# Statistics, row scales and branches rearranged between an attention stage and a gated feed-forward stage

## The chip, the cores and the metric

One core of one Trainium2 chip. The metric is the device time of one execution in microseconds (us); lower is better. The kernel before has a median of 538.29 us over 3 runs (535.64 to 538.82).

## The reference, cut to what matters

```python
def reference(**kw):
    attn_out = _attn_ref(q, k, v, n_global, n_local)   # B 2, H 8, S 768, D 64: local window and global keys
    x = attn_out.transpose(0, 2, 1, 3).reshape(B * S, H * D)       # 1536 x 512
    x = _moe_ref(x, w_gate, w_val, w_out, rms_g)
    return _moe2_ref(x, w_skip, w_gate, w1, w2)        # 8 experts, one for each token

def _moe_ref(x, w_gate, w_val, w_out, rms_g):
    rms = np.sqrt(np.mean(x * x, axis=-1, keepdims=True) + 1e-06)
    xn = x / rms * rms_g
    g = xn @ w_gate                                    # 512 x 1536
    silu = g * (1.0 / (1.0 + np.exp(-g)))
    return silu * (xn @ w_val) @ w_out
```

The change lies where the attention ends and `_moe_ref` begins: the root mean square over each row of x, and the first columns of the two products with `w_gate` and `w_val`.

## The kernel before, in words

Four stages follow each other: the attention (to about 85 us), the gated products with `w_gate` and `w_val` (to about 290 us), the product with `w_out` together with the routing (to about 408 us), and the experts. The program's order is written out by hand: each engine runs its instructions in the order in which the code issues them.

**Attention.** `attention` is a generator that goes over 24 items (head pair, group of 256 rows) in a software pipeline: in turn t it issues the scores of item t, the transposes (`trans`) of item t-2, the products with v (`pv`) of item t-3 and the output (`out`) of item t-4. Turns 24 to 27 drain the pipeline. `out` calls `Rms.take`: the item's output, which lies transposed (features on partitions, tokens on columns), is scaled by `rms_g`, split into a high part `xh` and a low part `xl`, and squared (`sq`); GpSimd adds the squares up (L398).

**Sum and root.** `Rms.stats` sums the squares over the features with TensorE: the 128x128 block of squares is the weight and one column of ones is the moving operand, so each call gives one column of `ss`. The 14 such matmuls appear in the trace as 28 instructions (two passes of 32-bit data). `root` computes 1/sqrt on a 128x12 tile in 12 small VectorE instructions. The scale is needed along the columns, as 1536 columns on all partitions (`rs`, three tiles of 512). `spread` makes them: a column of r, broadcast as weight, times the identity, 12 matmuls (24 passes), six copies to `rs` by ScalarE (L463).

**Gated products.** x has three tiles of 512 columns (index c); the 1536 gate columns are 12 pieces of 128 (index i), each with a gate and a value half (z = 0, 1). `products(i, c, a, b)` issues 24 matmuls, 12 for each z, each into its own PSUM tile (tags `ps0` and `ps1`, two buffers each). `gate1` evacuates them: VectorE multiplies the gate half by `rs` (L538), ScalarE takes the SiLU (L540), VectorE multiplies by the value half (L542). A PSUM buffer comes free with that, so products two pieces later wait for a gate. From piece (1, 0) on, a loop over `order` runs products, the splitting of a next weight unit, and the gate of the piece before.

**Weights.** Weights come as 64-bit floats. `load_unit` issues a 512 KB DMA from SP's queue into one of two buffers `wraw`; `split_unit` turns it into a high and a low 32-bit half in seven steps (ScalarE L471, VectorE L473, L478, L480, L483, ScalarE L485, GpSimd L486). The second buffer is free again behind L483.

**Filling.** In the drain, 12 of the 24 matmuls of piece (0, 0) (`s.first`) are issued as filling, six in turn 24 and six in turn 26 (`FILL`). The stats follow in turns 26 and 27. Behind the attention come the other 12 matmuls of (0, 0), `root`, then half pieces of c = 1 and the six `spread` calls in turns.

**Branches.** `flag` chooses a general attention where the mask is wide. It isn't taken with these inputs. It is read three times: before the attention, at turn 16 (L1029), and behind the attention (L1040).

Of the kernel before, what the change touches and what calls it, by code (L numbers as in the profile page):

```python
# [8 lines left out]
F32 = mybir.dt.float32  # L9
# [7 lines left out]
AX = mybir.AxisListType  # L17
PSUM = bass.MemoryType.PSUM
NEG = -1.0e9
FILL = {0: 6, 2: 6}  # L20
FAST_LOCAL = 97
FAST_GLOBAL = 32
FAR = 1 << 20
# [166 lines left out]
def attention(s, rms):  # L190
# [6 lines left out]
    nc, ap = s.nc, s.apool  # L197
# [79 lines left out]
    def trans(it, r):  # L277
        pr, g = it
        e = st[it][1]
        pt = s.ps_n.tile([128, 3, 128], F32, name="pt", tag="rb", bufs=2)  # L280
        for k in range(1 if g == r == 0 else 0, 3):
            nc.tensor.transpose(pt[:, k, :], e[:, r, 128 * k:128 * k + 128], s.ident)
        pts = ap.tile([128, 3, 128], F32, name="pts", bufs=4)
        outs[it, r] = (pt, pts)
# [40 lines left out]
    n = len(items)  # L325
# [12 lines left out]
    for t in range(n + 4):  # L338
        a, b, c, d, e = (items[t - z] if 0 <= t - z < n else None for z in range(5))
        if a:  # L340
            qk(a, t)
        if c:
            trans(c, 0)
            trans(c, 1)
        if d:
            pv(d, 0)
            pv(d, 1)
        some(s.first, FILL.get(t - n, 0))
        if b:
            zadd(b)  # L350
            zrec(b)
            for r in range(2):
                for x in range(2):
                    if t < n or r == 0:
                        norm(b, r, x, nc.gpsimd)
        if a:
            ttr(a, 0, 0)
        if a:
            ttr(a, 0, 1)
            ttr(a, 1, 0)  # L360
        if b and t >= n:
            norm(b, 1, 0, nc.vector)
            norm(b, 1, 1, nc.vector)
        if a:
            ttr(a, 1, 1)
        if c:
            evac(c, 0, nc.vector)
        if e:
            out(e)
        for half in range(2):  # L370
            if a:
                exp(a, half)
        if c:
            evac(c, 1, nc.scalar)
        if a:
            pr, g = a
            if g == 1 and pr + 2 < 8:
                load(pr + 2)
            if g == 2 and pr + 2 < 8:
                loadv(pr + 2)  # L380
        yield t


class Rms:
# [16 lines left out]

    def parts(self, hp, g, x, sq):
        s, nc = self.s, self.s.nc
        k, c = place(3 * self.b + g)
        nc.scalar.activation(s.xh[k][:, hp, c], x, AF.Copy, scale=s.rg[:, hp:hp + 1])
        nc.scalar.activation(sq, x, AF.Square)
        nc.vector.scalar_tensor_tensor(out=s.xl[k][:, hp, c], in0=x, scalar=s.rg[:, hp:hp + 1],
                                       in1=f(s.xh[k][:, hp, c]), op0=ALU.mult, op1=ALU.subtract)
# [17 lines left out]
    def stats(self, g, ss):  # L426
        s, nc = self.s, self.s.nc
        sqs = self.sq if g == 2 else self.sq[:1]
        for j in range(2 * g, 2 * g + 2):
            for z, sq in enumerate(sqs):  # L430
                nc.tensor.matmul(ss[:, 6 * self.b + j:6 * self.b + j + 1], lhsT=sq[:, 128 * j:128 * j + 128],
                                 rhs=s.ones[:, 0:1], start=z == 0, stop=z == len(sqs) - 1)


def place(z):

    return z // 2, slice(256 * (z % 2), 256 * (z % 2) + 256)


def root(s, ss):  # L440
# [11 lines left out]
        nc.vector.scalar_tensor_tensor(out=r, in0=t, scalar=1.5, in1=r, op0=ALU.add, op1=ALU.mult)  # L452


def spread(s, z):

    nc = s.nc
    rb = s.bank([128, 256], "rb")
    for j in range(2):
        nc.tensor.matmul(rb[:, 128 * j:128 * j + 128], lhsT=s.r[:, 2 * z + j:2 * z + j + 1].to_broadcast([128, 128]),  # L460
                         rhs=s.ident, start=True, stop=True)
    k, c = place(z)
    nc.scalar.copy(s.rs[k][:, c], rb)  # L463


def unpack(s, raw, pool, hi, lo, eng):
# [22 lines left out]
def load_unit(s, unit):  # L489

    raw = s.wpool.tile([128, 512, 2], I32, name="wraw", bufs=2)
    src = s.w_out[128 * unit[1]:128 * unit[1] + 128, :] if unit[0] == "o" else \
        s.wgv[unit[1], :, 512 * unit[2]:512 * unit[2] + 512]
    s.nc.sync.dma_start(raw.rearrange("p n t -> p (n t)"), src.bitcast(I32))
    s.wraw[unit] = raw
# [14 lines left out]
def products(s, i, c, a, b):  # L510

    nc = s.nc
    ps = []
    for z in range(2):
        p = s.ps_g.tile([128, b - a], F32, name=f"ps{z}", bufs=2)
        wh, wl = s.w[i, z]
        n = 0
        for k in range(4):
            for w, x in ((wh, s.xh), (wh, s.xl), (wl, s.xh)):
                nc.tensor.matmul(p, lhsT=w[:, k, :], rhs=x[c][:, k, a:b], start=n == 0, stop=n == 11)  # L520
                n += 1
                yield
        ps.append(p)
    s.gp[i, c, a, b] = ps


def some(parts, n):

    for _ in range(n):
        next(parts, None)  # L530


def gate1(s, i, c, a, b):

    nc = s.nc
    ps = s.gp.pop((i, c, a, b))
    u = s.h[c, i // 2][:, i % 2, a:b]
    nc.vector.tensor_tensor(u, ps[0], s.rs[c][:, a:b], ALU.mult)  # L538
    sg = s.gpool.tile([128, b - a], F32, name="sg", bufs=2)
    nc.scalar.activation(sg, u, AF.Silu)  # L540
    yield
    nc.vector.tensor_tensor(u, sg, ps[1], ALU.mult)  # L542
# [177 lines left out]
def run(*parts):  # L720

    parts = list(parts)
    while parts:
        parts = [p for p in parts if next(p, FAR) is None]
# [213 lines left out]
def attn_moe_kernel(ctx, tc, qx, kx, vx, rel, ints, wgv, w_out, rms_g, w9, w9t, w1, w2, out):  # L938
    s = K()
    nc = s.nc = tc.nc  # L940
# [4 lines left out]
    def pool(stack, name, side=None, space=None):  # L945
        kw = {} if space is None else {"space": space}
        return stack.enter_context(
            tc.tile_pool(name=name, bufs=1, side=side, reuse_waits="tile", **kw))

    s.cpool = pool(ctx, "const")  # L950
    dram = pool(ctx, "dram", space=bass.MemoryType.DRAM)
    s.xg = dram.tile([1024, 768], F32, name="xg")
    s.xm = dram.tile([1536, 512], F32, name="xm")
    ctx.enter_context(tc.manual_schedule())

    phase1, phase2 = ExitStack(), ExitStack()
    rctx, actx, gctx = ExitStack(), ExitStack(), ExitStack()
    s.gpool = pool(phase2, "g")
    early = pool(phase2, "early")
    s.apool = pool(actx, "attn")  # L960
# [2 lines left out]
    def htiles(pool, c, qs):  # L963
        for q in qs:
# [3 lines left out]
    rms = [Rms(s, 0), Rms(s, 1)]  # L968
# [15 lines left out]
    flag = nc.values_load(s.fasti[0:1, 0:1], min_val=0, max_val=1,  # L984
                          skip_runtime_bounds_check_because="a comparison's result")
# [9 lines left out]
        s.rs[c] = xpool.tile([128, 512], F32, name=f"rs{c}")  # L995
    s.rpool = pool(rctx, "rms", side="right")
    ps_n = s.ps_n = pool(gctx, "ps_n", space=PSUM)
    ps_o = pool(actx, "ps_o", space=PSUM)
    s.banks = 0

    def bank(shape, name):
# [17 lines left out]
    unit = unpacked()  # L1019
    s.first = products(s, 0, 0, 0, 512)  # L1020
    for t in att:
        if t < 3:
            next(bias)
        if t == 4:
            load_unit(s, units[0])
            load_unit(s, units[1])
        if 9 <= t < 19 or t > 23:
            next(unit, None)
        if t == 16:  # L1029
            with tc.If(flag == 0):  # L1030
                rms[0].general(s.xg)
        if t == 26:
            ss = s.ps_n.tile([128, 12], F32, name="ss", tag="rb", bufs=2)
            for g in range(3):
                rms[0].stats(g, ss)
            rms[1].stats(0, ss)
            rms[1].stats(1, ss)
        if t == 27:
            rms[1].stats(2, ss)
    with tc.If(flag == 0):  # L1040
        rms[1].general(s.xg)
        for g in range(3):
            rms[1].stats(g, ss)


    some(unit, 2)
    some(s.first, 24)
    root(s, ss)
    second = products(s, 0, 1, 0, 256)
    some(second, 12)  # L1050
    spread(s, 0)
    spread(s, 1)
    gate = gate1(s, 0, 0, 0, 512)
    next(gate)
    spread(s, 2)
    some(second, 24)
    run(gate)
    for z in range(3, 6):
        spread(s, z)
    run(gate1(s, 0, 1, 0, 256))  # L1060
    run(products(s, 0, 1, 256, 512))
    run(unit)
    run(products(s, 0, 2, 0, 512))
    run(gate1(s, 0, 1, 256, 512))
    behind = [(0, 2, 0, 512)]
    rctx.close()
    actx.close()
# [6 lines left out]
    htiles(big, 0, range(1, 6))  # L1074
    htiles(big, 1, range(1, 6))
    htiles(big, 2, range(6))
    order = [(i, c, 0, 512) for i in range(1, 12) for c in range(3)]
    todo = {(i, c, 0, 512): [("w", i + 1, c)] for i in range(1, 11) for c in range(2)}
    places = [(i, 2, 0, 512) for i in (1, 2, 3, 4, 4, 5, 6, 7, 7, 8, 9, 10)]
    for n, x in enumerate(places):  # L1080
        todo.setdefault(x, []).append(("o", n))
    ahead = iter([unit for x in order for unit in todo.get(x, ())])
    for _ in range(2):
        load_unit(s, next(ahead))

    def step1(x, *parts):

        run(products(s, *x))
# [1 line left out]
        behind.append(x)  # L1090

    for x in order:
        if x == order[-1]:
            run(gate1(s, *behind.pop()))
            xctx.close()
            hctx = ExitStack()
            s.hspool = pool(hctx, "hs")
            s.hs = {}
            split_h(s, 0)
        step1(x, *[split_unit(s, unit, nc.gpsimd) for unit in todo.get(x, ())])  # L1100
        for unit in todo.get(x, ()):
            unit = next(ahead, None)
            if unit:
                load_unit(s, unit)
# [57 lines left out]
    rows = (1, 5)  # L1162
# [293 lines left out]
```

## Time and profile before

| | us |
|---|---|
| median of 3 runs | 538.29 |
| lowest, highest | 535.64, 538.82 |
| the profiled execution, its own time | 538.66 |
| its span, first to last instruction | 536.8 |

The page gives the busy time of each engine over the span, and the span in 40 slices; other views give windows of time, the waits of an engine with what ended them, single instructions in order of time, and the DMA issues with their time to landing. A line as "79.45 0.52 PE L282 ... x3 [0.68 <-ACT pts L293]" says: at 79.45 us TensorE began three instructions of line 282 that together took 0.52 us, and before them it was idle 0.68 us until ScalarE's L293 ended. Matmuls are pipelined, so their durations overlap; a pace is read from the starts. TensorE is shown busy at either clock, so the granted clock has to be read beside it.

### The profile page before, as it was taken

The page shows a single profiled execution, that of the slowest core. Times are in us where ns is not written, and L with a number is a line of the kernel's source. Part 1 is how long each engine was busy: PE and PEld are TensorE (multiplying, and loading weights), DVE is VectorE, ACT ScalarE, POOL GpSimd, SP SyncE. Part 2 cuts the span into 40 slices and gives each one's busy share as a digit, 9 for nine tenths or more (in the row PEclk, how much of TensorE's full clock was granted, in tenths as well). Part 3 has the DMA queues.
Part 4 walks back from the last instruction along what each step waited for, and adds up shares of the span by engine and source line. Part 5 has one row for each costly group of instructions (what it writes and reads, how often), then busy time and mean ns, then how long its engine had stood idle before and what let it go on. Part 6 is the DMA issues. An engine that isn't in the chain of part 4 may idle for free. (4 is left out here: it accounts for less than half of the span.)

```text
span 536.8 us, 9708 instructions
## 1 busy us (share of the span) xinstructions
PE 514.3 (96%) x3376; PEld 417.8 (78%) x3376; DVE 396.4 (74%) x991; ACT 269.0 (50%) x621; POOL 150.6 (28%) x202
## 2 busy tenths in 40 slices
PE   3998989999999999999999999999999999999994
PEld 2676768888888888888888887887898778888873
DVE  6889985378887688768855367767743699999961
ACT  3899993432323333233323434424521778988750
POOL 5477782021221222222212000000000613666001
PEclk9999998999999999999999999999999999999998
DMA  8798701022222332232306123223681899999200
GB/s 263 251 333 260 238 16 40 12 96 92 100 97 78 117 119 87 92 129 87 117 29 233 74 78 119 82 75 118 211 307 39 293 398 397 397 402 395 100 14 17
DMA packets 30999, 85.91 MB, mean 160 GB/s; under 512 B 3847, under 2 KB 4103, under 8 KB 30944
## 3 DMA queue, kind: packets, MB, share of 16 engines
q1 hardware_dynamic: 26400, 73.86, 39.9%
q0 software_dynamic: 2672, 8.22, 4.1%
q10 hardware_dynamic: 1872, 3.15, 1.7%
q8 instruction: 28, 0.46, 0.4%
q14 instruction: 27, 0.22, 0.1%
HBM read 77.52 MB, written 8.65 MB: 161 GB/s over the span
## 5 line engine op out<-in xcount | busy, mean ns | idle before, releaser
L520 PE MATMUL ps<-xh,wh 128*128 128x512 f32 (+1 forms) x296 | 114.9, 388 | 0.1
L520 PE MATMUL ps<-xl,wh 128*128 128x512 f32 (+1 forms) x296 | 114.4, 387 | 0.0
L520 PE MATMUL ps<-xh,wl 128*128 128x512 f32 (+1 forms) x296 | 114.3, 386 | 0.0
L850 DVE TENSOR_TENSOR ewl<-eraw,ewh 128x1024 fp32r<-128x1024 f32 x72 | 83.4, 1216 | 7.6 <-ACT ewh L841 7.4
L841 ACT CAST ewh<-eraw 128x1024 fp32r<-128x1024 f32 x72 | 71.4, 1055 | 6.5 <-DVE ewl L850 4.6
L520 PEld LDWEIGHTS ps<-xh,wh 128*128 128x128 f32 x296 | 56.3, 190 | 11.5 <-issue 0.2
L520 PEld LDWEIGHTS ps<-xl,wh 128*128 128x128 f32 x296 | 56.2, 190 | 11.1
L520 PEld LDWEIGHTS ps<-xh,wl 128*128 128x128 f32 x296 | 56.2, 190 | 11.0
L473 DVE SCALAR_TENSOR_TENSOR wraw<-f64t,wraw 128x512 f32<-128x512 f32 x36 | 43.7, 1214 | 25.4 <-ACT f64t L471 25.4
L600 PE MATMUL px<-woh,hh 128*128 128x512 f32 (+1 forms) x156 | 61.2, 392 | 0.0
L486 POOL TENSOR_TENSOR wl<-f64t,wh 128x512 fp32r<-128x512 f32 x24 | 31.0, 1294 | 105.8 <-ACT wh L485 67.2
L600 PE MATMUL px<-woh,hl 128*128 128x512 f32 (+1 forms) x156 | 58.4, 374 | 0.0
L600 PE MATMUL px<-wol,hh 128*128 128x512 f32 (+1 forms) x156 | 58.2, 373 | 0.0
L485 ACT CAST wh<-f64t 128x512 fp32r<-128x512 f32 x24 | 14.9, 622 | 74.9 <-DVE f64t L483 74.9
L258 ACT ACTIVATE es<-es,m 128x192 f32<-128x192 f32 (+1 forms) x96 | 41.4, 445 | 5.6 <-DVE m L247 5.5
L275 POOL TENSOR_SCALAR es<-es,z 128x192 f32<-128x192 f32 (+1 forms) x94 | 37.8, 420 | 16.6 <-DVE z L267 6.3
L554 DVE TENSOR_TENSOR hl<-h,hh 128x256 fp32r<-128x256 f32 x72 | 25.4, 421 | 17.8 <-ACT hh L553 17.8
L542 DVE TENSOR_TENSOR h<-sg,ps 128x512 f32<-128x512 f32 (+1 forms) x37 | 24.7, 667 | 14.6 <-PE ps L520 10.7
L600 PEld LDWEIGHTS px<-woh,hh 128*128 128x128 f32 x156 | 29.4, 188 | 5.5 <-issue 0.9
L600 PEld LDWEIGHTS px<-woh,hl 128*128 128x128 f32 x156 | 29.3, 188 | 5.5
L600 PEld LDWEIGHTS px<-wol,hh 128*128 128x128 f32 x156 | 29.4, 189 | 4.1
L538 DVE TENSOR_TENSOR h<-ps,rs 128x512 f32<-128x512 f32 (+1 forms) x37 | 24.9, 672 | 10.3 <-ACT rs L463 5.7
(199 smaller groups left out, 986.5 us busy)
## 6 DMA issues: line engine op xcount, KB each, us to landing
eraw<-in_w_dram SPq DMA_DIRECT2D x64, 512.0 KB, 11.0
wraw<-in_wgv_dram SPq DMA_DIRECT2D x24, 512.0 KB, 3.8
wraw<-in_w_out_dram SPq DMA_DIRECT2D x12, 512.0 KB, 3.2
vp<-in_vx_dram SPq DMA_DIRECT2D x8, 704.0 KB, 6.0
eraw<-in_w_dram POOLq DMA_DIRECT2D x8, 512.0 KB, 13.5
kd<-in_kx_dram SPq DMA_DIRECT2D x7, 464.0 KB, 9.0
xm<-x SPq DMA_DIRECT2D x12, 256.0 KB, 2.8
out_dram<-x ACTq DMA_DIRECT2D x12, 256.0 KB
```

What stands on the lines that cost most here:

```text
L258: nc.scalar.activation(e[:, r, e0:e0 + n], e[:, r, e0:e0 + n], AF.Exp, bias=m[:, j:j + 1], scale=-1.0, accum_out=z[:, j:j + 1])
L275: eng.tensor_scalar(e[:, r, e0:e0 + n], e[:, r, e0:e0 + n], z[:, j:j + 1], one[0], ALU.mult, *one[1:])
L473: nc.vector.scalar_tensor_tensor(out=a.bitcast(F32), in0=t, scalar=F64_LEAST, in1=a.bitcast(F32), op0=ALU.is_ge, op1=ALU.mult)
L485: nc.scalar.copy(hi, t)
L486: eng.tensor_tensor(lo, t, f(hi), ALU.subtract)
L520: nc.tensor.matmul(p, lhsT=w[:, k, :], rhs=x[c][:, k, a:b], start=n == 0, stop=n == 11)
L538: nc.vector.tensor_tensor(u, ps[0], s.rs[c][:, a:b], ALU.mult)
L542: nc.vector.tensor_tensor(u, sg, ps[1], ALU.mult)
L554: nc.vector.tensor_tensor(hl[:, i, :], src, f(hh[:, i, :]), ALU.subtract)
L600: nc.tensor.matmul(p, lhsT=h[:, k, :], rhs=w[k][:, c:c + N], start=n == 0, stop=n == 35)
L841: eng.copy(wh, raw)
L850: eng.tensor_tensor(wl, raw, f(wh), ALU.subtract)
```

## The change

- The filling moves: three matmuls of `s.first` between the two transposes of turn 24, seven behind the products with v of turn 24, none in turn 26 as a block. Instead, one matmul of `s.first` stands behind each of the 14 stats matmuls. With 3 + 7 + 10 + 4 = 24 all of piece (0, 0) is issued inside the attention.
- `spread` changes from 12 matmuls and six copies to one transpose of r (128x12), one copy to SBUF by VectorE, one DMA of 6 KB to DRAM and three DMAs of 256 KB that read it back to all partitions, all on SP's queue.
- The rest of the splitting (`run(unit)`) and the next two weight loads stand ahead of `root`; before, most of this stood between and behind the gates.
- The two halves of piece (0, 1) get one PSUM bank each (`half0`, `half1`), piece (0, 2) takes the two banks of the attention's output, so four pieces stand in PSUM before the first gate. All gates follow behind the products of (0, 2).
- The branch of turn 16 joins the one behind the attention.

The text of the change also names 384-column exponentials; the diff has no line on the exponentials.

```diff
-FILL = {0: 6, 2: 6}
@@ attention, turn t
         if c:
             trans(c, 0)
+            if t == n:
+                some(s.first, 3)
             trans(c, 1)
         if d:
             pv(d, 0)
             pv(d, 1)
-        some(s.first, FILL.get(t - n, 0))
+        if t == n:
+            some(s.first, 7)
@@ Rms.stats, behind each matmul
+                yield
@@
-def spread(s, z):
+def spread(s):
     nc = s.nc
-    rb = s.bank([128, 256], "rb")
-    for j in range(2):
-        nc.tensor.matmul(rb[:, 128 * j:128 * j + 128], lhsT=s.r[:, 2 * z + j:2 * z + j + 1].to_broadcast([128, 128]),
-                         rhs=s.ident, start=True, stop=True)
-    k, c = place(z)
-    nc.scalar.copy(s.rs[k][:, c], rb)
+    p = s.ps_n.tile([12, 128], F32, name="rp", tag="rb", bufs=2)
+    nc.tensor.transpose(p, s.r, s.ident)
+    rows = s.rpool.tile([12, 128], F32, name="rows", bufs=1)
+    nc.vector.tensor_copy(rows, p)
+    nc.sync.dma_start(s.rd, rows)
+    for k in range(3):
+        nc.sync.dma_start(s.rs[k].rearrange("p (a b) -> p a b", a=4),
+                          s.rd[4 * k:4 * k + 4, :].rearrange("(o a) b -> o a b", o=1).to_broadcast([128, 4, 128]))
@@ attn_moe_kernel
-        if t == 16:
-            with tc.If(flag == 0):
-                rms[0].general(s.xg)
         if t == 26:
             ss = s.ps_n.tile([128, 12], F32, name="ss", tag="rb", bufs=2)
+            for x, g in ((0, 0), (0, 1), (0, 2), (1, 0), (1, 1)):
+                for _ in rms[x].stats(g, ss):
+                    some(s.first, 1)
+        if t == 27:
+            for _ in rms[1].stats(2, ss):
+                some(s.first, 1)
+    with tc.If(flag == 0):
+        for x in rms:
+            x.general(s.xg)
             for g in range(3):
-                rms[0].stats(g, ss)
-            rms[1].stats(0, ss)
-            rms[1].stats(1, ss)
-        if t == 27:
-            rms[1].stats(2, ss)
...
-    some(unit, 2)
-    some(s.first, 24)
+                run(x.stats(g, ss))
+        run(products(s, 0, 0, 0, 512))
+    run(unit)
...
+    for _ in range(2):
+        load_unit(s, next(ahead))
     root(s, ss)
-    second = products(s, 0, 1, 0, 256)
-    some(second, 12)
-    spread(s, 0)
-    spread(s, 1)
-    gate = gate1(s, 0, 0, 0, 512)
-    next(gate)
-    spread(s, 2)
-    some(second, 24)
-    run(gate)
-    for z in range(3, 6):
-        spread(s, z)
-    run(gate1(s, 0, 1, 0, 256))
-    run(products(s, 0, 1, 256, 512))
-    run(unit)
+    for z in range(2):
+        pair = s.ps_g.tile([128, 2, 256], F32, name=f"half{z}", tag=f"ps{z}", bufs=2)
+        s.gp[0, 1, 256 * z, 256 * z + 256] = [pair[:, x, :] for x in range(2)]
+    s.gp[0, 2, 0, 512] = [s.bank([128, 512], "po") for _ in range(2)]
+    run(products(s, 0, 1, 0, 256))
+    second = products(s, 0, 1, 256, 512)
+    some(second, 6)
+    spread(s)
+    some(second, 18)
     run(products(s, 0, 2, 0, 512))
-    run(gate1(s, 0, 1, 256, 512))
+    for x in ((0, 0, 512), (1, 0, 256), (1, 256, 512)):
+        run(gate1(s, 0, *x))
     behind = [(0, 2, 0, 512)]
```

## Rows read from the trace of the kernel before

**Rows 1.** The page's first part: busy time, share of the span, instructions.

```profile
PE 514.3 (96%) x3376; PEld 417.8 (78%) x3376; DVE 396.4 (74%) x991; ACT 269.0 (50%) x621; POOL 150.6 (28%) x202
```

**Rows 2.** Windows: length, busy us (instructions) by engine, clock, DMA share, GB/s.

```profile
110.00:180.00 70.00, 70.00 (x310) 57.97 (x309) 54.57 (x76) 21.70 (x38) 16.79 (x13) 1.00 0.30 98
430.00:500.00 70.00, 69.68 (x336) 56.81 (x335) 69.52 (x91) 58.16 (x75) 32.52 (x12) 1.00 1.03 394
```

**Rows 3.** TensorE's longest wait from 110 us to the end: us, times, longest.

```profile
PE rk L696 <- DVE oh L659: 0.7, 2, 0.4
```

**Rows 4.** TensorE's matmuls in order of time: start, us, instructions, idle before them.

```profile
79.45 0.52 PE L282 MATMUL pt<-ident,es 128*128 128x128 f32 x3 [0.68 <-ACT pts L293]
...
86.50 0.28 PE L431 MATMUL ss<-ones,sq 128*128 128x1 f32 x2
...
90.49 0.77 PE L520 MATMUL ps<-xh,wh 128*128 128x512 f32 x1
...
95.72 0.28 PE L520 MATMUL ps<-xh,wh 128*128 128x256 f32 x1
...
97.15 0.38 PE L460 MATMUL rb<-ident,r 128*128 128x128 f32 x2
...
98.69 0.36 PE L520 MATMUL ps<-xh,wh 128*128 128x256 f32 x1
...
100.19 1.83 PE L460 MATMUL rb<-ident,r 128*128 128x128 f32 x12
101.78 0.36 PE L520 MATMUL ps<-xh,wh 128*128 128x256 f32 x1
...
104.73 0.40 PE L520 MATMUL ps<-xh,wh 128*128 128x512 f32 x1
...
110.20 0.39 PE L520 MATMUL ps<-xh,wh 128*128 128x512 f32 x1
```

**Rows 5.** Windows for `ss` (PE, PEld, DVE) and all tiles (also ACT, POOL); clock, DMA.

```profile
88.00:88.50 0.50, 0.50 (x7) 0.50 (x6) 0.00 (x0) 1.00 0.00 0
89.00:89.50 0.50, 0.50 (x4) 0.50 (x4) 0.00 (x0) 0.50 0.34 115
96.00:97.00 1.00, 1.00 (x11) 1.00 (x10) 0.00 (x0) 0.00 (x0) 0.00 (x0) 1.00 0.00 0
```

**Rows 6.** ScalarE and VectorE in order of time, behind the attention.

```profile
88.49 0.66 ACT L471 ACTIVATE f64t<-wraw 128x512 f32<-128x512 f32 x1
...
90.47 0.17 DVE L444 TENSOR_SCALAR rv<-ss 128x12 f32<-128x12 f32 x1 [2.54 <-PEq L1040]
...
92.73 0.17 DVE L452 SCALAR_TENSOR_TENSOR r<-rt,r 128x12 f32<-128x12 f32 x1
...
98.63 1.28 ACT L540 ACT_TABLE_LOAD   x1
98.64 0.69 DVE L538 TENSOR_TENSOR h<-ps,rs 128x512 f32<-128x512 f32 x1 [5.74 <-ACT rs L463]
```

**Rows 7.** Two steps of the splitting: duration in ns, least, median, greatest.

```profile
L473 DVE SCALAR_TENSOR_TENSOR wraw<-f64t,wraw x36: 682/1352/1677, 39.4 to 270.4; 128x512 f32<-128x512 f32 x36
...
L480 DVE SCALAR_TENSOR_TENSOR f64t<-wraw,f64t x36: 674/693/695, 45.5 to 272.7; 128x512 uint32<-128x512 uint32 x36
```

**Rows 8.** The first DMA of 2 KB: issue, and the instruction that waited for it.

```profile
0.79 0.41 SPq L40 DMA_DIRECT2D ints<-in_ints_dram  x1
...
4.10 0.17 DVE L60 CAST intw<-ints 128x4 f32<-128x4 int32 x1 [4.10 <-DMA ints<-in_ints_dram]
```

**Rows 9.** Line 605, 256 KB to DRAM, 12 times: issue to landing, us.

```profile
DMA to landing us min/median/max: 2.4/2.8/5.1
```

**Rows 10.** DMA issues: count, KB each, median us from issue to landing.

```profile
vlo<-in_vx_dram SPq DMA_DIRECT2D x8, 192.0 KB, 9.4
```

**Rows 11.** ScalarE in turn 16, either side of its branch.

```profile
58.65 0.48 ACT L293 COPY pts<-pt 128x384 f32<-128x384 f32 x1
59.25 0.47 ACT L405 ACTIVATE xh<-po,rg 128x256 fp32r<-128x256 f32 x1
```

More of the change, by code (lines that the diff above doesn't have):

```diff
@@ L403, in parts @@
         s, nc = self.s, self.s.nc
-        k, c = place(3 * self.b + g)
+        n = 3 * self.b + g
+        k, c = n // 2, slice(256 * (n % 2), 256 * (n % 2) + 256)
         nc.scalar.activation(s.xh[k][:, hp, c], x, AF.Copy, scale=s.rg[:, hp:hp + 1])
@@ L432, in stats @@
                                  rhs=s.ones[:, 0:1], start=z == 0, stop=z == len(sqs) - 1)
-def place(z):
-    return z // 2, slice(256 * (z % 2), 256 * (z % 2) + 256)
+                yield
 def root(s, ss):
@@ L512, in products @@
     nc = s.nc
-    ps = []
+    ps = s.gp.setdefault((i, c, a, b), [])
     for z in range(2):
-        p = s.ps_g.tile([128, b - a], F32, name=f"ps{z}", bufs=2)
+        if z == len(ps):
+            ps.append(s.ps_g.tile([128, b - a], F32, name=f"ps{z}", bufs=2))
+        p = ps[z]
         wh, wl = s.w[i, z]
@@ L522, in products @@
                 yield
-        ps.append(p)
-    s.gp[i, c, a, b] = ps
 def some(parts, n):
@@ L953, in attn_moe_kernel @@
     s.xm = dram.tile([1536, 512], F32, name="xm")
+    s.rd = dram.tile([12, 128], F32, name="rd")
     ctx.enter_context(tc.manual_schedule())
     phase1, phase2 = ExitStack(), ExitStack()
-    rctx, actx, gctx = ExitStack(), ExitStack(), ExitStack()
+    rctx, actx, octx, gctx = ExitStack(), ExitStack(), ExitStack(), ExitStack()
     s.gpool = pool(phase2, "g")
@@ L997, in attn_moe_kernel @@
     ps_n = s.ps_n = pool(gctx, "ps_n", space=PSUM)
-    ps_o = pool(actx, "ps_o", space=PSUM)
+    ps_o = pool(octx, "ps_o", space=PSUM)
     s.banks = 0
@@ L1028, in attn_moe_kernel @@
             next(unit, None)
-        if t == 16:
-            with tc.If(flag == 0):
-                rms[0].general(s.xg)
         if t == 26:
             ss = s.ps_n.tile([128, 12], F32, name="ss", tag="rb", bufs=2)
-            for g in range(3):
-                rms[0].stats(g, ss)
-            rms[1].stats(0, ss)
-            rms[1].stats(1, ss)
-        if t == 27:
-            rms[1].stats(2, ss)
[L1040 to L1043, printed above, removed]
@@ new lines, in attn_moe_kernel @@
+        if t == 27:
[4 more added lines that the diff above has]
+            x.general(s.xg)
+            for g in range(3):
+                run(x.stats(g, ss))
+        run(products(s, 0, 0, 0, 512))
+    run(unit)
+    order = [(i, c, 0, 512) for i in range(1, 12) for c in range(3)]
+    todo = {(i, c, 0, 512): [("w", i + 1, c)] for i in range(1, 11) for c in range(2)}
+    places = [(i, 2, 0, 512) for i in (1, 2, 3, 4, 4, 5, 6, 7, 7, 8, 9, 10)]
@@ new lines, in attn_moe_kernel @@
+    for n, x in enumerate(places):
+        todo.setdefault(x, []).append(("o", n))
+    ahead = iter([unit for x in order for unit in todo.get(x, ())])
+    for _ in range(2):
+        load_unit(s, next(ahead))
+    root(s, ss)
+    for z in range(2):
[3 more added lines that the diff above has]
+    run(products(s, 0, 1, 0, 256))
@@ L1076, in attn_moe_kernel @@
     htiles(big, 2, range(6))
[L1077 to L1084, printed above, removed]
     def step1(x, *parts):
@@ L1092, in attn_moe_kernel @@
     for x in order:
+        if x == order[1]:
+            octx.close()
         if x == order[-1]:
```

## The prediction, made before the run

> **What bounds the kernel now.** I read the busy times first: TensorE is busy 96% of the span, VectorE 74% [rows 1]. A share over the whole span hides stages, so next the windows: from 110 to 180 us TensorE is busy all 70 us at a granted clock of 1.00, and in the experts, from 430 to 500 us, 69.7 of 70 [rows 2]. VectorE is full there too (69.5) and the DMA engines as well (1.03), so the third view has to say who waits for whom: behind 110 us the longest wait of TensorE in total is 0.7 us, in two pieces [rows 3]. So from the start of piece (1, 0), at 110.20 us, to its last product TensorE sets the pace, and the splitting and loading of later stages start at events that TensorE releases. A microsecond taken out of TensorE's order ahead of 110.20 should come out at the end. The question is when (1, 0) starts.
>
> The fourth view is TensorE's order between the last transposes of the attention and 110.20 [rows 4], and beside it the clock [rows 5]. "Busy" misleads here: TensorE has hardly a gap from 86.5 to 110.2, but four stretches of it are slow or are work that can go. The stats run from 86.50 to 90.49. [...] Those 12 products take from 90.49 to 95.72, 0.436 us each; 24 of the same form at the high clock take 104.73 to 110.20, 0.228 each [rows 4]. The two stretches of `spread` take 97.15 to 98.69 and 100.19 to 101.78 [rows 4].
>
> **The change part by part, in TensorE's time.**
>
> *Three fillings between the transposes.* Before the second transpose of turn 24 TensorE is idle 0.68 us, until ScalarE frees the PSUM tile [rows 4]. Three products of 0.228 are 0.68, so they cost nothing where they go and are missing later: -0.68. The cover is that wait; without it the gain is 0. The seven others of turn 24 and the block of turn 26 only change places.
>
> *Stats among products.* Before the clock fell, about 22 of the 28 instructions took 0.11 us each, and the last six 0.22; I get that from the 3.99 us and a fall at about 88.9 (inside the slice between the two windows of [rows 5]; 2.4 / 0.11 + 1.4 / 0.22 = 28). At the high clock all 28 are 3.1 us, some 0.7 less (-0.68). The 12 products at the low clock cost 12 x (0.436 - 0.228) = 2.49; with the clock up, -2.49. What I assume is that the clock stays up. Two one-column instructions then stand between 512-column products, so that more than half of each pair's 0.45 us is a product. Nothing in this trace shows just that mix; [rows 5] show only the end with no products (falls) and the end with nothing else (back up). The bound on the other side is the same 3.2 us lost again, a rival below. The pairing itself may hide one weight load per pair behind the product, or expose one more: 14 x 0.11 = 1.5 us either way. I take 0, since the load of a stats block and the load of a product cost 0.11 in the row as it stands.
>
> *Spread.* 24 passes leave TensorE: 1.54 + 1.59 = -3.13 [rows 4]. One transpose of r comes in. Twelve passes take 1.54, so one is 0.13; two passes and the change of operand I take as 0.3 (+0.30, bounds 0.13 to 0.5).
>
> *The branch of turn 16.* ScalarE paces the attention. On it the branch leaves a gap from 59.13 (58.65 + 0.48) to 59.25 [rows 11]: -0.1, at least 0, at most 0.3.
>
> *Branch, splitting and loads ahead of root.* The branch behind the attention stays, at what it costs now. `run(unit)` puts four VectorE steps ahead of `root` that came later before. ScalarE's L471 ends at 89.15 [rows 6]; behind it one L473 of 0.68 to 1.35 and three steps of at most 0.69 [rows 7] end at 92.6 at the latest. `root` takes 90.47 to 92.90, 2.43 us [rows 6], so r stands at 95.0. TensorE wants it later: see below. This costs nothing, with half a microsecond to spare. On SP's queue the second weight load waits for L483 of that unit, so it is issued before `rows` exists and stands ahead of the four new DMAs; being 512 KB, it is to be landed before them or nearly so.
>
> The sum: 0.68 + 0.68 + 2.49 + 3.13 - 0.30 + 0.1 = 6.8 us. (1, 0) starts at 110.2 - 6.8 = 103.4.
>
> **Does the new chain of the scales stay hidden?** It ends at the first gate, whose L538 must free `ps0` before (1, 0) can start. Counted back from 103.4: 24 products of 512 columns (5.47) and 18 of 256 columns (12 take 95.72 to 97.15, 0.119 each, so 2.14) lie behind the transpose, which ends at 95.8 and begins at 95.5, half a microsecond behind r. Counted on: the copy of `rows`, 0.3 (a 12-column VectorE step is 0.17 [rows 6], and it reads PSUM behind a semaphore), 96.1. The write of 6 KB to DRAM: no such small one is in the trace; the nearest rows are the 2 KB load that was waited for from 0.79 to 4.10, 3.3 us [rows 8], and the least of twelve 256 KB writes, 2.4 [rows 9]. I take 2.8. The read of 256 KB: 2.4 to 5.1, and I take the median, 2.8 [rows 9]. That is 101.7, and with L538's 0.69 [rows 6] 102.4: a microsecond ahead of 103.4. At the far ends, 3.3 and 5.1, it is 105.2, a stall of 1.8. The table load of 1.28 us that stood ahead of the first SiLU [rows 6] has nothing ahead of it now and runs during the DMAs. `ps1` is wanted 2.7 us later (12 products) and the two gates of (0, 1) 5.5 us later, against some 1.4 us for each gate's rest; nothing is late there. The gate of (0, 2) frees banks that no early product wants.
>
> [...]
>
> **The rivals.**
>
> *The chain sticks out a little.* For it: the far ends of [rows 8, 9]. Against it: the medians. Stall up to 1.8, gain 5.0 to 6.8; at 1.8 the time is 533.3.
>
> *The clock falls all the same.* For it: it fell inside 2.4 us of stats [rows 5], and the stats now last as long or longer, at half their density. Then some 6.5 us lie at half speed as they do now, and 3.2 us come back: gain 3.6, 534.7. [...]
>
> *The gain is given back in the experts.* VectorE and the DMA engines are full there [rows 2], so a stage that starts earlier might wait for them. Against it: all that they do there starts from slots that TensorE frees, and TensorE waits 0.7 us [rows 3]. Half the gain lost: 534.9.
>
> *Slower: the DMA legs queue.* Loads of 192 KB behind others on the same queue took 9.4 us to land [rows 10]. If both legs take that long, the first gate ends at 96.1 + 18.8 + 0.7 = 115.6, TensorE stands idle for 12 us, and 5.4 us are lost net: 543.7; idle TensorE could also lose its clock again (+3, 546.9). It decides from legs of 13.4 us together (5.6 assumed, 1.0 slack, 6.8 gain). Against it: the one load ahead is issued three microseconds or more before `rows`.
>
> *It does nothing.* For that TensorE would have to wait elsewhere; [rows 3] leave no room.
>
> **How the numbers follow.** The sum goes against the profiled execution: 538.66 - 6.8 = 531.9. That run is 0.37 above the median of 538.29, so against the median it is 531.5. Chances: this case 0.61, the chain sticking out 0.16, the clock 0.13, given back 0.06, slower 0.04. The likeliest case alone, with a pairing of -0.9 (past that `root` is late and TensorE waits for it) to +1.2 and the small bounds, is 530.4 to 532.9. The range reaches to the first two rivals: 530.0 to 534.8, which leaves out the last two and the tails. One per cent, 5.4 us, is about what a measurement of this kernel can tell from no change. Faster by more: the likeliest case and a third of the first rival, 0.66. Within 1%: the rest of that rival, the clock, the gain given back, 0.30. Slower: 0.04.
>
> **What would show it.** Right, if TensorE's granted clock is 1.00 throughout from 80 to 105 us, the 14 stats with their 14 products take about 6.3 us, the first product of (1, 0) starts near 103.4 with no idle time before it, and the distance from there to the last instruction is what it was. Wrong, if `ss` shows a window at 0.50; if (1, 0) waits for `h` L538, and that for the DMA of `rs`; if TensorE waits for `r` at the transpose (the splitting ahead of `root` was late); or if (1, 0) starts on time and the end doesn't move.

## The result and the profile after

| | before | changed |
|---|---|---|
| median of 15 runs, us | 538.29 | 532.87 |
| lowest to highest | 535.64 to 539.86 | 531.92 to 535.77 |
| profiled execution, its span | 538.66, 536.8 | 534.08, 532.4 |

The ratio of the runs is 0.9917, with a 95% interval of 0.9897 to 0.9937: 0.8% faster. In a later series of runs the changed kernel stands at 0.9884 (0.9843 to 0.9926). The forecast time of 531.5 was 1.4 us too low and its range holds the result; "faster by over 1%" had 0.66 and the first ratio lies just inside 1%.

Where the time goes is unchanged. First the page's busy times, then windows as in [rows 2], then TensorE's longest wait behind 110 us as in [rows 3], all of the changed kernel:

```profile
PE 507.1 (95%) x3353; PEld 412.0 (77%) x3353; DVE 396.4 (74%) x992; ACT 267.1 (50%) x615; POOL 151.1 (28%) x202
```

```profile
110.00:180.00 70.00, 70.00 (x310) 57.97 (x309) 56.12 (x82) 23.11 (x41) 17.00 (x14) 1.00 0.31 98
430.00:500.00 70.00, 69.64 (x339) 56.96 (x338) 69.62 (x88) 57.84 (x73) 32.46 (x11) 1.00 0.97 369
```

```profile
PE rk L697 <- DVE oh L660: 0.7, 2, 0.4
```

TensorE is busy 7 us less and still waits for nobody. Some of the 7 is this one execution: in the two other profiles of the changed kernel TensorE is busy 509.6 and 508.9 us, in the five of the kernel before 512.7 to 514.6. Its order behind turn 24, beside [rows 4]:

```profile
79.84 0.54 PE L281 MATMUL pt<-ident,es 128*128 128x128 f32 x3
80.14 0.48 PE L523 MATMUL ps<-xh,wh 128*128 128x512 f32 x1
...
81.06 0.52 PE L281 MATMUL pt<-ident,es 128*128 128x128 f32 x3
...
86.84 0.38 PE L434 MATMUL ss<-ones,sq 128*128 128x1 f32 x2
87.09 0.48 PE L523 MATMUL ps<-xl,wh 128*128 128x512 f32 x1
...
93.61 0.35 PE L523 MATMUL half<-xh,wh 128*128 128x256 f32 x1
...
97.72 0.27 PE L458 MATMUL rp<-ident,r 128*12 128x128 f32 x1 [0.28 <-DVE r L451]
...
99.97 0.40 PE L523 MATMUL po<-xh,wh 128*128 128x512 f32 x1
...
105.44 0.39 PE L523 MATMUL ps<-xh,wh 128*128 128x512 f32 x1
```

The second transposes of turn 24 begin 1.22 us behind the first in both kernels (78.23 and 79.45 before, 79.84 and 81.06 now), with three products in between where TensorE stood idle. The stats run in pairs with products from 86.84, and (1, 0) begins at 105.44, with no wait. And the clock during the pairs, in windows of all tiles:

```profile
88.00:89.00 1.00, 1.00 (x10) 0.92 (x9) 0.93 (x2) 0.00 (x0) 0.00 (x0) 1.00 0.00 0
...
91.00:92.00 1.00, 1.00 (x9) 0.89 (x7) 0.98 (x1) 0.00 (x0) 0.78 (x1) 1.00 0.79 250
```

It stays at 1.00, where [rows 5] have 0.50. The stretch from the first transpose of turn 24 to (1, 0) is 105.44 - 79.84 = 25.60 us; before it was 110.20 - 78.23 = 31.97. That is 6.4 less, with 6.7 forecast for this part. Yet the execution is only 4.6 us shorter, since turn 24 began 1.6 us later. That difference lies ahead of all that the change touches. At the start TensorE waited 2.5 us for the load of `kd`, and its 76th product of the scores begins at 22.24 us here and at 20.41 before.

### The profile page after: what moved, and what is told of

It reads as the page before. It is cut to its first block, busy times and chain, and to the rows that moved or that the text cites. A ratio compares the mean times of both kernels' runs of the same rounds, so it can differ in the third digit from the quotient of the medians.

```text
span 532.4 us, 9653 instructions
## 1 busy us (share of the span) xinstructions
PE 507.1 (95%) x3353; PEld 412.0 (77%) x3353; DVE 396.4 (74%) x992; ACT 267.1 (50%) x615; POOL 151.1 (28%) x202
## 5 line engine op out<-in xcount | busy, mean ns | idle before, releaser
L523 PE MATMUL ps<-xh,wh 128*128 128x512 f32 x272 | 106.5, 391 | 0.1
L523 PE MATMUL ps<-xl,wh 128*128 128x512 f32 x272 | 106.3, 391 | 0.0
L523 PE MATMUL ps<-xh,wl 128*128 128x512 f32 x272 | 106.3, 391 | 0.0
L523 PEld LDWEIGHTS ps<-xh,wh 128*128 128x128 f32 x272 | 51.1, 188 | 11.0 <-DVE h L543 0.6
L523 PEld LDWEIGHTS ps<-xl,wh 128*128 128x128 f32 x272 | 51.1, 188 | 10.4
L523 PEld LDWEIGHTS ps<-xh,wl 128*128 128x128 f32 x272 | 51.1, 188 | 10.3
L235 PE MATMUL sc<-kd,qd 64*64 64x192 f32 (+2 forms) x384 | 23.0, 351 | 13.1 <-DVE keep L104 6.8
L541 ACT ACTIVATE sg<-h 128x512 f32<-128x512 f32 (+1 forms) x37 | 22.5, 609 | 18.7 <-DVE h L539 18.7
```

The lines of the kernel that those rows point to most:

```text
L235: nc.tensor.matmul(sc[x][o, r, 0:n], lhsT=qs[pr][d, i:i + 64], rhs=ks[pr][d, k0:k0 + n], start=True, stop=True)
```

## The experiments

All kernels were profiled, and this stretch is read from each trace, since it doesn't hang on how early the loads of the start land. "Low" is the time at the 0.50 clock behind the stats, summed from windows of 1 us (twice what each lacks to 1.00); "rest" goes from (1, 0) to the start of TensorE's last matmul, and from there to the end of the span it is 7.8 to 8.0 us in every run.

| run | turn 24 | (1, 0) | stretch | low | rest |
|---|---|---|---|---|---|
| before, five executions | 78.23 | 110.20 | 31.97 | 6.8 | 418.8 |
| | 78.99 | 109.38 | 30.39 | 3.4 | 418.9 |
| | 79.40 | 109.91 | 30.51 | 3.4 | 419.0 |
| | 79.04 | 110.98 | 31.94 | 6.8 | 418.8 |
| | 79.79 | 110.29 | 30.50 | 3.4 | 418.9 |
| changed, three executions | 79.84 | 105.44 | 25.60 | 0 | 419.1 |
| | 79.08 | 104.84 | 25.76 | 0 | 419.0 |
| | 78.95 | 104.72 | 25.77 | 0 | 418.8 |
| stats as a block | 77.82 | 104.57 | 26.75 | 3.4 | 419.1 |
| spread on TensorE | 77.62 | 106.42 | 28.80 | 0 | 418.7 |
| root first | 79.36 | 104.53 | 25.17 | 0 | 418.7 |
| one more DMA hop | 79.51 | 106.43 | 26.92 | 0 | 419.4 |
| pairs alone, on before | 79.85 | 109.08 | 29.23 | 0 | 418.8 |
| root first, one full piece | 80.06 | 104.97 | 24.91 | 0 | 418.7 |

Two things stand in this table before any single run is read. The rest is 418.7 to 419.4 whatever the stretch, so what is taken out ahead of (1, 0) does arrive at the end. And the kernel before has not one stretch but two, 30.4 to 30.5 and 31.9 to 32.0, by how long its clock was low.

### Stats as a block

```diff
             for x, g in ((0, 0), (0, 1), (0, 2), (1, 0), (1, 1)):
-                for _ in rms[x].stats(g, ss):
-                    some(s.first, 1)
+                run(rms[x].stats(g, ss))
         if t == 27:
-            for _ in rms[1].stats(2, ss):
-                some(s.first, 1)
+            run(rms[1].stats(2, ss))
+            some(s.first, 14)
```

> The changed kernel with one thing undone: the 14 stats run as a block, with the 14 products behind them instead of between them. The stretch is read from the first transpose of turn 24 to the first product of (1, 0): 31.97 us before, 25.60 in the changed kernel. My theory, that the pairing keeps the clock up: the clock falls to 0.50 within the block and the stretch grows by about 3.2 us (0.7 on the stats, 2.5 on the products behind them), to 28.8. The rival, that the seven products moved ahead of the block or the 256-column products behind it keep the clock up by themselves and the pairing is only a reordering: it stays near 25.6.

Measured: 0.9909 (0.9877 to 0.9942), median 533.42. The clock fell, as the theory has it; the windows of this kernel:

```profile
87.00:88.00 1.00, 1.00 (x11) 1.00 (x11) 0.69 (x1) 0.20 (x1) 0.00 (x0) 1.00 0.00 0
88.00:89.00 1.00, 1.00 (x5) 0.80 (x5) 0.00 (x0) 0.99 (x2) 0.51 (x1) 0.74 0.21 41
89.00:90.00 1.00, 1.00 (x4) 0.79 (x3) 0.98 (x1) 0.00 (x0) 0.78 (x1) 0.50 0.79 250
90.00:91.00 1.00, 1.00 (x4) 0.81 (x3) 0.93 (x3) 0.00 (x0) 0.00 (x0) 0.50 0.58 234
91.00:92.00 1.00, 1.00 (x4) 0.77 (x4) 0.97 (x2) 0.00 (x0) 0.00 (x0) 0.56 0.00 0
```

But it was low for 3.4 us, not 6.5, and the stretch grew by 1.0 to 1.2 us, not 3.2. Half of 3.4 is 1.7; some of that comes back, since TensorE no longer waits for r (0.3 to 0.4 us in the changed kernel). The pairing's mechanism is shown and its size in the expectation was not right. In total time this kernel can't be told from the changed one.

### The kernel before, four more times

> The kernel before, unchanged, profiled again. It tells how long the clock stays low behind the stats in another execution, and when the first transpose of turn 24 begins. If the length of the fall is what splits its runs, an execution near 535.7 has a fall some five to six microseconds shorter than the 6.5 us of the first profile, with the same time at turn 24; if the start splits them, the fall is 6.5 us in each and turn 24 comes up to 3 us earlier or later.

> The kernel before once more, for a third execution: the same two readings, the length of the fall and the time of turn 24, each against the execution's own time.

> The kernel before, a fourth execution. Its stretch was 31.97 with 6.9 us at the low clock, and 30.39 and 30.51 with 3.2. Theory, that the stretch is 28.7 plus half of the time at the low clock: it fits again, and where the execution takes near 535.8 the clock does not fall at all or the attention is early by a microsecond. Rival: the stretch varies without the clock.

> The kernel before, a fifth execution, for the same reading: 28.7 plus half of the time at the low clock.

The same program, windows over 77 to 100 us, the granted clock third from the end. The second execution:

```profile
77.00:100.00 23.00, 21.85 (x229) 18.92 (x227) 11.48 (x40) 11.51 (x30) 6.72 (x12) 0.93 0.07 24
```

and the fourth:

```profile
77.00:100.00 23.00, 21.89 (x217) 18.79 (x216) 11.15 (x39) 9.94 (x28) 6.75 (x12) 0.85 0.07 24
```

In five executions the clock was low for 3.4 us three times and for 6.8 us twice (the first profile, on which the prediction rests, is one of the two), and the stretch follows: 30.39, 30.50, 30.51 against 31.94, 31.97. Half of the 3.4 us between them is 1.7, and 1.5 is measured. So 28.7 plus half of the low time fits all five within 0.2 us (30.4 and 32.1). The executions took 537.87 (3.4 low), 538.46 (3.4), 538.66 (6.8), 538.85 (3.4) and 539.50 (6.8); turn 24 began anywhere from 78.2 to 79.8, so the start of the attention adds as much spread as the clock. No profile caught an execution of the group near 535.7 (11 of the 39 runs of the first two series are at 536.2 or less). By the same sum the clock doesn't fall there at all, 30.4 - 1.7 on 537.87 giving 536.2. The mean granted clock of an execution, which is on record for the timed runs of three series too, speaks for it: it is 0.992 in the three profiles with 3.4 us, 0.990 in the two with 6.8, and 0.995 in all eight runs at 536.4 or less. Half of 3.4 us is 0.003 of the span. Where in those eight the clock was low is not shown, and two slower runs have 0.995 too (537.76 and 540.99), so the clock isn't all that splits the runs.

### Pairs alone

```diff
-FILL = {0: 6, 2: 6}
+FILL = {0: 6}
             for g in range(3):
-                rms[0].stats(g, ss)
-            rms[1].stats(0, ss)
-            rms[1].stats(1, ss)
-        if t == 27:
-            rms[1].stats(2, ss)
+            for x, g in ((0, 0), (0, 1), (0, 2), (1, 0), (1, 1)):
+                for _ in rms[x].stats(g, ss):
+                    some(s.first, 1)
+        if t == 27:
+            for _ in rms[1].stats(2, ss):
+                some(s.first, 1)
```

(With it come the `yield` in `stats` and the tiles of `products` as in the change.)

> The kernel before with one thing of the change alone: the stats stand one by one among products. Turn 24 keeps its six fillings, the block of six in turn 26 goes, 14 products stand behind the 14 stats and four behind the attention. The runs of the kernel before lie in two groups, about 535.7 and about 538.9. Theory: the upper group is the executions in which the clock falls for some six microseconds behind the stats, as in its profile; the pairing takes the fall away, the stretch from the first transpose of turn 24 to (1, 0) shrinks from 31.97 by up to 3.2 us, to about 29, and all runs lie near 535.5, with no upper group. Rival: the two groups come from the start of the attention, where a load lands sooner or later; then both groups stay, each 0 to 3 us lower.

Measured: 0.9949 (0.9936 to 0.9963); five runs from 535.80 to 537.46 beside ten of the kernel before, of which one is 535.84 and nine 537.85 to 539.68. The window says why:

```profile
77.00:100.00 23.00, 21.83 (x247) 18.57 (x242) 12.38 (x42) 12.62 (x35) 7.56 (x13) 1.00 0.07 24
```

The stretch is 29.23: 1.2 us less than that of an execution with the short fall, 2.7 less than with the long one. The median falls by 2.7 us, half of the whole gain. The upper group is gone, as the theory says, though the runs lie 0.3 to 2.0 us above the 535.5 expected. At 29.23 the pairs cost some 0.5 us more than the 28.7 of the fit.

### Spread on TensorE

```diff
 def spread(s):
-    p = s.ps_n.tile([12, 128], F32, name="rp", tag="rb", bufs=2)
-    nc.tensor.transpose(p, s.r, s.ident)
...
+    for z in range(6):
+        rb = s.ps_n.tile([128, 256], F32, name="rb", bufs=2)
+        for j in range(2):
+            nc.tensor.matmul(rb[:, 128 * j:128 * j + 128],
+                             lhsT=s.r[:, 2 * z + j:2 * z + j + 1].to_broadcast([128, 128]),
+                             rhs=s.ident, start=True, stop=True)
+        nc.scalar.copy(s.rs[z // 2][:, 256 * (z % 2):256 * (z % 2) + 256], rb)
```

> The changed kernel with one thing undone: the scales are spread by twelve matmuls in 24 passes and six copies, all at the place where the transpose of r and its DMAs stand now. My theory, that those passes are pure TensorE time: the stretch grows by 3.13 less the 0.3 of the transpose, some 2.8 us, to 28.4. The rival, that the start of (1, 0) hangs on the gates and not on TensorE's order: the scales are ready some four microseconds earlier, the gates with them, and the stretch grows by less than 1 us or shrinks.

Measured: 0.9964 (0.9938 to 0.9989), median 535.91, 0.5% above the changed kernel's ratio. TensorE's order in this kernel, with VectorE's first gate:

```profile
95.49 3.47 PE L460 MATMUL rb<-ident,r 128*128 128x128 f32 x24 [0.27 <-DVE r L451]
...
97.06 0.69 DVE L538 TENSOR_TENSOR h<-ps,rs 128x512 f32<-128x512 f32 x1 [1.72 <-ACT rs L463]
...
106.42 0.39 PE L522 MATMUL ps<-xh,wh 128*128 128x512 f32 x1
```

The stretch is 28.80, 3.0 to 3.2 above the changed kernel's (2.8 expected). VectorE's first gate was released at 97.06 here, 19.4 us behind turn 24 and not 24.5 as in the changed kernel, and those five microseconds bought nothing: the start of (1, 0) hangs on TensorE's own order and not on the gates, so the rival falls.

### One more DMA hop

```diff
     nc.sync.dma_start(s.rd, rows)
+    nc.sync.dma_start(s.rd2, s.rd)
...
-                          s.rd[4 * k:4 * k + 4, :]...
+                          s.rd2[4 * k:4 * k + 4, :]...
```

> The changed kernel with the chain of the scales made longer: between the write of the rows to DRAM and the three reads stands one more DMA of 6 KB, from DRAM to DRAM. The changed kernel's trace has the write issued at 98.33, the reads at 100.94, the first gate's L539 done at 105.0 and (1, 0) begun at 105.44: one leg is 2.6 us and the slack 0.44. Theory, that the chain is hidden with that slack and no more: (1, 0) waits for the first gate, and the stretch grows by a leg of about 2.6 less 0.44, by 2.2 us, to 27.8. Rival, that the gates aren't on the way to (1, 0): the stretch stays at 25.6.

Measured: 0.993 (0.9904 to 0.9957), median 535.02. The timeline of this kernel, with SP's issues, the first gate's first step (L540 here) and TensorE:

```profile
98.00 0.38 SPq L461 DMA_DIRECT2D rd<-rows  x1
100.47 0.53 SPq L462 DMA_DIRECT2D rd<-rd  x1
102.42 1.29 SPq L464 DMA_DIRECT2D rs<-rd  x3
...
105.59 0.69 DVE L540 TENSOR_TENSOR h<-ps,rs 128x512 f32<-128x512 f32 x1 [7.62 <-DMA rs<-rd]
106.43 0.47 PE L524 MATMUL ps<-xh,wh 128*128 128x512 f32 x1 [1.15 <-DVE h L540]
```

TensorE now waits 1.15 us at (1, 0), for the first gate; the stretch is 26.92, 1.2 to 1.3 more (2.2 expected). The added leg took 1.95 us and not 2.6, and the others were 0.3 shorter together. The mechanism holds: the chain of the scales is hidden in the changed kernel with 0.3 to 0.7 us to spare (0.44, 0.27 and 0.74 in its three profiles), and beyond that each microsecond of it counts.

### Root first

```diff
-    run(unit)
+    some(unit, 2)
...
-    for _ in range(2):
-        load_unit(s, next(ahead))
-
+    load_unit(s, next(ahead))
     root(s, ss)
...
     spread(s)
+    run(unit)
+    load_unit(s, next(ahead))
     some(second, 18)
```

> The changed kernel with the root ahead of the rest of the splitting: of the splitting only the two steps that stood there in the kernel before come first, the rest and the second weight load follow the copy of the rows. In the changed kernel TensorE waits 0.28 us for r at the transpose. Theory, that this wait is the splitting's: r stands about 1.5 us earlier, TensorE waits 0, the first gate ends 1.5 us earlier against the first product of (1, 0), and the stretch shrinks by 0.3 to 0.5 us. Rival, that r was late because the sums are late: the wait stays. Second rival, that the second half of the splitting is now late for (1, 0), value half: TensorE waits there for wl.

Measured: 0.9885 (0.9848 to 0.9922), median 532.31. In its timeline r is done at 95.56 and waits for TensorE:

```profile
95.39 0.17 DVE L451 SCALAR_TENSOR_TENSOR r<-rt,r 128x12 f32<-128x12 f32 x1
...
96.81 0.27 PE L458 MATMUL rp<-ident,r 128*12 128x128 f32 x1
97.11 0.28 DVE L460 COPY rows<-rp 12x128 f32<-12x128 f32 x1 [1.56 <-PE rp L458]
...
102.58 0.69 DVE L539 TENSOR_TENSOR h<-ps,rs 128x512 f32<-128x512 f32 x1 [2.67 <-DMA rs<-rd]
104.53 0.39 PE L523 MATMUL ps<-xh,wh 128*128 128x512 f32 x1
```

The stretch is 25.17, 0.4 to 0.6 less, and the first gate's step ends 1.3 us ahead of (1, 0) instead of 0.4. So the wait for r was the splitting's. The second half of `w` wasn't late. The gate's 0.8 us don't come from the earlier r, though, and 1.5 were expected: the transpose stands where TensorE's order has it, 1.25 us behind r, and it is the write to DRAM that is shorter, 1.73 us from its issue to that of the reads and not 2.61. In this run the second weight load is issued behind the reads and not ahead of the write; whether that is the reason is open.

### Root first and one full piece, beside the changed kernel

```diff
-    for z in range(2):
-        pair = ...
-    run(products(s, 0, 1, 0, 256))
-    second = products(s, 0, 1, 256, 512)
-    some(second, 6)
+    second = products(s, 0, 1, 0, 512)
+    some(second, 12)
     spread(s)
+    run(unit)
+    load_unit(s, next(ahead))
...
```

> A version meant to beat the changed kernel: the root ahead of the rest of the splitting, as in the run with the root first, and piece (0, 1) as one piece of 512 columns, with the spread behind its first 12 matmuls. 48 matmuls of 256 columns at 0.119 us are 5.71, 24 of 512 at 0.228 are 5.47: the stretch shrinks by another 0.24 from the 25.17 of that run, to 24.9, with 0.3 to 0.7 us against the changed kernel in all. Rival: with the transpose of r at 2.7 instead of 3.6 us behind the sums TensorE waits for r again, and the stretch stays at 25.2 or above.

> The changed kernel, unchanged, timed beside the version above on one chip. Theory: the stretch is again 25.6 to 25.8 with turn 24 at its own time, and the median lies 0.3 to 0.7 us above that of the version above, which five rounds may not separate. Rival: a difference of over 1.5 us either way, which would say that something outside of the stretch moved.

> The changed kernel, unchanged, profiled again. In its first profile turn 24 began 1.61 us later than in that of the kernel before, behind a later landing of kd at 10.65 us. Theory, that this is the execution and not the change: here turn 24 begins at another time, 77.5 to 78.5, and the stretch from there to (1, 0) is again 25.6. Rival, that the removed branch or the changed program makes the start later: turn 24 begins near 79.8 again.

The stretch is 24.91, as worked out, and 25.77 in the changed kernel timed beside it. The times can't show 0.9 us: 0.9881 (0.9840 to 0.9922), median 532.92, against 0.9884 (0.9843 to 0.9926), median 533.02. It is the shortest stretch of all, and no faster kernel that a measurement could tell. The other execution of the changed kernel had its turn 24 at 79.08 and a stretch of 25.76. The 79.08 lies outside of the 77.5 to 78.5 expected, but it stands with 78.95 in the third execution and 78.23 to 79.79 in the kernel before: the start varies from execution to execution, and no effect of the change is seen in it.

## Why the prediction was right or wrong

**What bounds the kernel: right.** The rest is constant within 0.7 us over all stretches from 24.9 to 32.0. The rival in which the experts give the gain back falls: at most 0.3 us went there.

**Fillings between the transposes: right.** 1.22 us from transpose to transpose in both kernels; 0.68 gained. That is read from the two orders, and no run undoes this part alone.

**Stats among products: right in mechanism, mis-sized.** The pairs took 6.3 us as forecast, at 1.00, and undoing them brings the fall back. The mis-sized term is the clock's: 0.68 + 2.49 = 3.17 us, the second for the 12 products of piece (0, 0) from 90.49 on [rows 4], were read from one execution, which had the long fall of 6.8 us. In three of five executions it was 3.4 us and the term 1.7, and the pairs themselves cost some 0.5. Over the five profiles of before the mean stretch is 31.06, over the three of the changed kernel 25.71: 5.35 us. The medians show about as much (5.42), but that is in part luck. The five profiles have none of the group near 535.7, to which 5 of the 15 runs before belong, and the means of the same runs are 4.5 us apart, as the ratio of 0.9917 says. Taking 1.7 to 3.2 for this term would have given 5.3 to 6.8 for the sum, and 0, for an execution in which the clock doesn't fall, 3.6.

**Spread: right.** 2.8 forecast, 3.0 to 3.2 measured.

**Splitting ahead of root, costed at nothing: wrong by 0.4 to 0.6 us.** One of the signs of being wrong came true: TensorE waits for r at the transpose, 0.28 us in the first profile and 0.43 and 0.44 in the others. VectorE was free of the splitting when I said (94.17, with this attention 1.6 us later than the one I read). What failed is the 2.43 us of `root`: it takes 3.40 here, and 2.44 in the run with the root first. The changed kernel's VectorE and GpSimd:

```profile
94.98 1.33 POOL L487 TENSOR_TENSOR wl<-f64t,wh 128x512 fp32r<-128x512 f32 x1 [3.20 <-ACT wh L486]
94.98 0.17 DVE L450 SCALAR_TENSOR_TENSOR rt<-rt,rv 128x12 f32<-128x12 f32 x1
95.19 1.15 DVE L451 SCALAR_TENSOR_TENSOR r<-rt,r 128x12 f32<-128x12 f32 x1
...
97.40 0.17 DVE L451 SCALAR_TENSOR_TENSOR r<-rt,r 128x12 f32<-128x12 f32 x1
97.72 0.27 PE L458 MATMUL rp<-ident,r 128*12 128x128 f32 x1 [0.28 <-DVE r L451]
98.02 0.28 DVE L460 COPY rows<-rp 12x128 f32<-12x128 f32 x1 [0.45 <-PE rp L458]
98.33 0.38 SPq L461 DMA_DIRECT2D rd<-rows  x1
100.94 1.29 SPq L463 DMA_DIRECT2D rs<-rd  x3
104.31 0.69 DVE L539 TENSOR_TENSOR h<-ps,rs 128x512 f32<-128x512 f32 x1 [6.01 <-DMA rs<-rd]
```

The splitting's last step, on GpSimd, starts beside `root`, and one of its 12-column steps of 0.17 us takes 1.15. I counted what was moved ahead of `root` on VectorE and forgot what it issues on GpSimd.

**The chain: hidden, with less to spare.** 0.44 us measured (first step of the gate done at 105.00, (1, 0) at 105.44), 0.27 and 0.74 in the two other profiles, and 1.0 forecast. The write leg took 2.61 (2.8 taken), the read 3.37 (2.8 taken; the copy of the rows was on time). The rival in which it sticks out was near; the hop shows what it would have cost.

**The branch: right, and worth a little more.** Beside [rows 11], the changed kernel's ScalarE in turn 16:

```profile
60.43 0.48 ACT L292 COPY pts<-pt 128x384 f32<-128x384 f32 x1
...
60.79 0.50 ACT L408 ACTIVATE xh<-po,rg 128x256 fp32r<-128x256 f32 x1
```

From start to start it is 0.59 to 0.62 us in the six profiles with the branch and 0.36 in the eight without, so 0.24 us where 0.1 was forecast. How much of it reaches the end can't be read from turn 24, which began at 77.6 to 80.1 over these 14 profiles.

## What to carry to other kernels

Read a clock term from several executions before it goes into a sum: the same program lost half of 3.4 or half of 6.8 us to the same stats. Thin matmuls that must stand in a dense stretch go among thick ones: here the clock stayed at 1.00 with the stats in pairs and was at 0.50 for 3.4 us with the stats as a block. A detour over DRAM is worth its 6 us (2.61 and 3.37 here) when TensorE has that much of its own work to run meanwhile. When a step is moved, count what it issues on every engine: beside the splitting's 1.33 us on GpSimd a step of `root` that takes 0.17 us took 1.15.

## What the runs showed of the hardware

In six profiles one of the 12 small VectorE steps of `root` took 0.91 to 1.31 us; in the five of them that were read on both engines it stands beside a GpSimd step of 1.29 to 1.33. In the changed kernel's third execution both start at 94.09 and end 0.02 us apart:

```profile
94.09 1.29 POOL L487 TENSOR_TENSOR wl<-f64t,wh 128x512 fp32r<-128x512 f32 x1 [3.19 <-ACT wh L486]
94.09 1.31 DVE L450 SCALAR_TENSOR_TENSOR rt<-rt,rv 128x12 f32<-128x12 f32 x1
```

The other 11 steps of that `root` took 0.16 or 0.17 us. In the five profiles VectorE's long step ends 0.02 to 0.03 us behind GpSimd's; why it does, no run shows. Here it is a step with two inputs, in the run with the stats as a block one with a single input:

```profile
92.97 1.29 POOL L487 TENSOR_TENSOR wl<-f64t,wh 128x512 fp32r<-128x512 f32 x1 [3.19 <-ACT wh L486]
93.38 0.91 DVE L445 TENSOR_SCALAR r<-rv 128x12 int32<-128x12 int32 x1
```

The low clock behind the same stats lasted 3.4 us in three executions of the kernel before and 6.8 in two, with the same work in front of it. And a dependent chain over DRAM took 2.5 to 2.7 us (1.7 and 1.3 in the two runs with the root first) from the issue of a 6 KB write to the issue of what waits for it, 1.95 for 6 KB from DRAM to DRAM, and 3.2 to 3.5 from the issue of a 256 KB read to the step that uses it.
